# A windowed-attention and gated-MLP kernel on one core: where the Wo products stand, which steps carry the norms, and how the first loads are cut

## The chip, the cores and the metric

The kernel runs on one core of one Trainium2 chip. The metric is the device time of one execution in microseconds (us). Besides that time, one execution was recorded by the hardware profiler; its records are called the profile or the trace here.

## The reference

```
x  = A_x                                     # [2048, 512], bf16
xn = (x - mean(x)) / sqrt(var(x) + 1e-5)     # over the last axis
# A: causal attention with a window of 256 keys, 32 heads of 16
q, k, v = split(xn @ wqkv)                   # wqkv [512, 1536]
p  = softmax(q k^T / 4, masked where not 0 <= i - j < 256)
a  = (p v) @ wo                              # wo [512, 512]
# B: a gated product without a nonlinearity
b  = ((xn @ w_gate) * (xn @ w_up)) @ w_down  # F = 1792
out = x + a + b                              # [2048, 512]
```

B_x is not used.

## The kernel before, in words

The 2048 rows are cut into four chunks of 512, T = 0 to 3, and a chunk into four blocks of 128 rows, b = 0 to 3. All weights and x stay in SBUF. For a chunk the kernel makes the norm of its blocks, transposes them (`xnT`), projects V, K and Q (`vp`, `qkp`), makes gate and up products for 14 groups of 128 hidden columns (`gp`, `up`, and their product `hT`), the scores and exponentials of the attention, and the products of the weights with V (`acc`). The last two products add into one PSUM tile per block: `psd` takes 14 matmuls of `down` (L375: hT with Wd) and then four of `wo` (L381: OT with Wo, one for each group c of eight heads). `store` (L399) adds x on VectorE (DVE) and issues the copy to HBM.

The order is written out by the program itself. There are 76 score steps: 16 for chunk 0 and 20 for each later one, four or five steps for each pair (T, c). A step is `scores` (matmuls into the one S tile, L258; an exponential on ScalarE (ACT), L265; triangular masks on GpSimd (POOL), L137), then, where a pair (T, c) ended two steps earlier, `values` (the acc matmuls, L313, and two DVE transposes, L319) and `divide` (DVE: reciprocal, product L331, and the transpose L333 that writes `OT`), then `fill`, then `mask_diag` (DVE, L286).

`fill` takes the next items of a list, `fillers()`, as long as a budget lasts. The budget rises by 14.24 units with each step; a unit is about one matmul of 512 columns, scores cost 1.85 units, values 5.5. An item of the list may carry `after`: it may not be taken before that pair has been divided in an earlier step, and then the list stops:

```
cost, f, before, after = work[n]
if after is not None and after > valued:
    break
```

In chunk T the list holds, for b = 0 to 3, the `down` items of block b of chunk T-1 (seven items of two matmuls), `wo` with c = 0, 1, `wo` with c = 2, 3, and the store; then the gate and up items of chunk T and the projections of chunk T+1. Between the blocks stand the norm items of chunk T+1, at cost 0: `norm_stats` (DVE, L148, L149), `norm_scale` (POOL: `ve` L157, `rs` L159), `norm_apply` (DVE, L167), `norm_transpose` (a DMA transpose on the SP queue, L179). Chunk 1's norms stand between the gate and up items of chunk 0. PSUM has four banks for everything but the scores (tag M), among them `psd`, `acc`, `gp`, `up`, `vp`, `qkp`. A tile of that tag gets the bank that was freed first.

The start (`setup`, `first_chunk`): SP issues the loads of x block 0, block 1, blocks 2 and 3 together, then Wqkv in three parts of 512 columns (V, K, Q), then the other weights. TensorE (PE) multiplies an identity 42 times (`wps`, L89) while it has no data. DVE takes, in this order, the statistics of blocks 0 and 1, and then for each b the apply of block b and the statistics of block b + 2. POOL makes ve and rs. PE takes the transposes of block 0 (`xTp`, L183), and then for each b the transposes of block b + 1 and the V projection of block b. ACT copies each transposed block to `xnT` (L184) and each V block out of PSUM (L201).

Of the kernel before, what the change touches and what calls it, by code (L numbers as in the profile page):

```python
# [10 lines left out]
ACT = mybir.ActivationFunctionType  # L11
ALU = mybir.AluOpType
# [13 lines left out]
class Kernel:  # L26
# [26 lines left out]
    def setup(self):  # L53
        nc, const, NT, NF = self.nc, self.const, self.NT, self.NF
        self.x = const.tile([128, NT, 512], BF16, name="x")
        self.Wqkv = const.tile([128, 4, 1536], BF16, name="Wqkv")
        self.Wo = const.tile([128, 4, 512], BF16, name="Wo")
        self.Wg = const.tile([128, 4, self.F], BF16, name="Wg")
        self.Wu = const.tile([128, 4, self.F], BF16, name="Wu")
        self.Wd = const.tile([128, NF, 512], BF16, name="Wd")  # L60
        xv = self.x_d.rearrange("(t p) d -> p t d", p=128)
        wq = self.w_d["qkv"].rearrange("(k p) n -> p k n", p=128)
        wg = self.w_d["g"].rearrange("(k p) n -> p k n", p=128)
        wu = self.w_d["u"].rearrange("(k p) n -> p k n", p=128)
        for lo, hi in ((0, 1), (1, 2), (2, 4)):
            nc.sync.dma_start(out=self.x[:, lo:hi, :], in_=xv[:, lo:hi, :])
        for lo in (1024, 512, 0):
            nc.sync.dma_start(out=self.Wqkv[:, :, lo:lo + 512], in_=wq[:, :, lo:lo + 512])
        h = self.F // 2
        for lo in (0, h):  # L70
            nc.sync.dma_start(out=self.Wg[:, :, lo:lo + h], in_=wg[:, :, lo:lo + h])
            nc.sync.dma_start(out=self.Wu[:, :, lo:lo + h], in_=wu[:, :, lo:lo + h])
            if lo == 0:
                nc.sync.dma_start(out=self.x[:, 4:8, :], in_=xv[:, 4:8, :])
        nc.sync.dma_start(out=self.Wd[:], in_=self.w_d["d"].rearrange("(f p) n -> p f n", p=128))
        nc.sync.dma_start(out=self.Wo[:], in_=self.w_d["o"].rearrange("(c p) n -> p c n", p=128))
        nc.sync.dma_start(out=self.x[:, 8:NT, :], in_=xv[:, 8:NT, :])

        warm = const.tile([128, 1], F32, name="warm")
        nc.vector.memset(warm[:], 0.0)  # L80
        nc.scalar.activation(out=warm[:], in_=warm[:], func=ACT.Exp)
        ident = const.tile([128, 128], BF16, name="ident")
        nc.gpsimd.memset(ident[:], 0.0)
        nc.gpsimd.affine_select(out=ident[:], in_=ident[:], compare_op=ALU.not_equal, fill=1.0,
                                base=0, pattern=[[-1, 128]], channel_multiplier=1)
        self.ident = ident
        wps = self.ps_m.tile([128, 128], F32, tag="M", name="wps")
        for _ in range(42):
            nc.tensor.matmul(wps[:], lhsT=ident[:], rhs=ident[:], start=True, stop=True)  # L89
        pi = const.tile([128, 1], I32, name="pi")  # L90
        nc.gpsimd.iota(pi[:], pattern=[[0, 1]], base=0, channel_multiplier=1)
        podd = const.tile([128, 1], I32, name="podd")
        nc.vector.tensor_scalar(out=podd[:], in0=pi[:], scalar1=4, scalar2=1,
                                op0=ALU.arith_shift_right, op1=ALU.bitwise_and)
        self.odd = const.tile([128, 1], F32, name="odd")
        nc.vector.tensor_copy(out=self.odd[:], in_=podd[:])
        self.mhalf = const.tile([128, 4], F32, name="mhalf")
        nc.gpsimd.memset(self.mhalf[:], -0.5)
        self.diag = const.tile([128, 64], BF16, name="diag")
        self.far = const.tile([128, 64], BF16, name="far")  # L100
        nc.gpsimd.memset(self.diag[:], BIG)
        nc.gpsimd.memset(self.far[:], BIG)
        for half in (slice(0, 64), slice(64, 128)):
            self.triangle(self.diag[half], True)
            self.triangle(self.far[half], False)
        self.xnT, self.Q, self.hT, self.O, self.OT = {}, {}, {}, {}, {}
        self.K, self.Ko, self.V, self.VS = {}, {}, {}, {}
        self.strips, self.at = {}, {}
# [43 lines left out]
    def norm_scale(self, t, n=4):  # L152

        nc = self.nc
        mv = self.stats[t][0]
        ve = self.small.tile([128, n], F32, tag="ve", name="ve")
        nc.gpsimd.tensor_scalar(out=ve[:], in0=mv[:, :, 1], scalar1=1e-5, scalar2=None, op0=ALU.add)  # L157
        rs = self.small.tile([128, n], F32, tag="rs", name="rs")
        nc.gpsimd.tensor_tensor(out=rs[:], in0=ve[:], in1=self.mhalf[:, 0:n], op=ALU.pow)  # L159
        for u in range(t, t + n):  # L160
            self.stats[u][2] = rs
# [9 lines left out]
    def norm_transpose(self, t, by_dma):  # L171

        nc = self.nc
        xn = self.xns.pop(t)
        T, b = divmod(t, 4)
        if b == 0:
            self.xnT[T] = self.chunk2.tile([128, 4, 4, 128], BF16, tag="xnT", name=f"xnT{T}")
        if by_dma:
            nc.sync.dma_start_transpose(out=self.xnT[T][:, b, :, :], in_=xn[:])  # L179
            return  # L180
        ps = self.ps_m.tile([128, 4, 128], BF16, tag="M", name="xTp")
        for k in range(4):
            nc.tensor.transpose(ps[:, k, :], xn[:, 128 * k:128 * k + 128], self.ident[:])  # L183
        nc.scalar.activation(out=self.xnT[T][:, b, :, :], in_=ps[:], func=ACT.Copy)  # L184

    def bank(self, ks, name):

# [37 lines left out]
    def first_chunk(self):  # L225

        self.new_chunk(0)
        for b in range(2):
            self.norm_stats(b, 1)
            self.norm_scale(b, 1)  # L230
        for b in range(4):
            self.norm_apply(b)
            if b < 2:
                self.norm_stats(b + 2, 1)
                self.norm_scale(b + 2, 1)
        self.norm_transpose(0, False)
        for b in range(4):
            if b < 3:
                self.norm_transpose(b + 1, False)
            self.proj_v(b)  # L240
        self.proj_qk(0, 0, 1)
        self.proj_qk(0, 0, 0, on_act=True)
        self.swap_halves(0, self.nc.scalar)
        self.proj_qk(0, 1, 1)
# [158 lines left out]
    def fillers(self):  # L403


        out = []
# [30 lines left out]
        def norms(T, at, step):  # L437

            t, out = 4 * T, {}
            for b in range(4):  # L440
                for k, f in enumerate((lambda b=b: self.norm_stats(t + b, 1),
                                       lambda b=b: self.norm_scale(t + b, 1),
                                       lambda b=b: self.norm_apply(t + b),
                                       lambda b=b: self.norm_transpose(t + b, True))):
                    out.setdefault(at + step * b + (0, 0, 1, 1)[k], []).append((0, f))
            return out

        def down(T, b):
            for lo in range(0, NF, 2):
                add(2, lambda lo=lo: self.down(T, b, lo, lo + 2))  # L450

        def wo(T, b, cs):
# [3 lines left out]
        for c in range(2, 4):  # L456
            qk(0, c, self.first[0, c])
        for T in range(NCH):
            todo = {}
            if T:  # L460
                todo = norms(T + 1, 0, 1) if T + 1 < NCH else {}
                for b in range(4):
                    for g in todo.get(b, ()):
                        add(*g)
                    down(T - 1, b)
                    wo(T - 1, b, (0, 1))
                    wo(T - 1, b, (2, 3))
                    add(0, lambda T=T, b=b: self.store(T - 1, b))
            for g in todo.get(4, ()):
                add(*g)  # L470
            gu(T, norms(1, 1, 3) if T == 0 else {})
            if T + 1 < NCH:
                project(T + 1)
# [9 lines left out]
    def run(self):  # L483
# [12 lines left out]
                    steps.append((T, c, pieces))  # L496
        due = {g: key for key, g in self.last.items()}
        SCORES, VALUES = 1.85, 5.5
        work = self.fillers()
        total = sum(w[0] for w in work) - RESERVE + SCORES * len(steps) + VALUES * (len(due) - 1)  # L500
        spent, n, scored = 0, 0, 0
# [29 lines left out]
        for g, s in enumerate(steps):  # L531
            fill(-1, g)
            valued = ready
            self.scores(*s)
            scored = spent
            spent += SCORES
            upto = total * (g + 1) / len(steps)
            if values(g - LAG):
                fill(min(spent + 4, upto), g)
                divide(g - LAG)  # L540
            if g < len(steps) - 1:
                fill(upto, g)
                self.mask_diag(*s)
# [57 lines left out]
```

The softmax here doesn't subtract the row's maximum and nothing guards it: scores larger than these inputs give would overflow.

## Time and profile before

| what | value |
|---|---|
| median of 3 runs | 273.40 us (273.21 to 273.44) |
| the profiled execution's own time | 273.34 us |
| its span, first to last instruction | 271.6 us |
| PE busy | 261.7 us, 96% of the span |
| DVE, ACT, POOL busy | 182.3, 170.6, 113.4 us |
| granted TensorE clock, mean | 1.000 |

The span leaves out what lies before the first and after the last instruction: 273.34 - 271.6 = 1.74 us. Times in the trace are counted from the start of the span. Matmuls overlap: one of 512 columns is recorded with about 380 ns, while the next starts 215 ns after it (four vp matmuls are recorded with 1.02 us together). So the ends of PE work are modelled, and an idle time after a matmul is recorded somewhat shorter than the time that was lost.

### The profile page before, as it was taken

Reading aid. Unit: us, or ns where it says so; the run is one execution under the profiler, and the core shown is the slowest. Engines: PE = TensorE matmul, PEld = TensorE weight load, DVE = VectorE, ACT = ScalarE, POOL = GpSimd, SP = SyncE. Lnnn points to the kernel's source line nnn. Section 1 sums busy time; section 2 is a strip of 40 time slices with the busy share of each in tenths; the row PEclk is TensorE's granted clock in tenths of the full one; section 3 lists DMA queues with packets and bytes.
Section 4 is the critical chain, followed back from the end, with each engine's and each line's share of the span. In section 5 each row is a group of like instructions: output and inputs, shape, how many; then the busy total and the mean of one; then the engine's idle time right before and its main releaser. Section 6 shows DMA issues by size and latency. Waiting matters only on the chain.

```text
span 271.6 us, 8888 instructions
## 1 busy us (share of the span) xinstructions
PE 261.7 (96%) x3886; PEld 120.2 (44%) x3886; DVE 182.3 (67%) x351; ACT 170.6 (63%) x131; POOL 113.4 (42%) x282
## 2 busy tenths in 40 slices
PE   7999999999799999999989999999999999999993
PEld 6444444444344444444434444444444444444452
DVE  5377998876845959676665868857662675969160
ACT  3666757686456676769655676768765666675400
POOL 6123333434545443345545543545443354443400
PEclk9999999999999999999999999999999999999999
DMA  6999911110021100001012110000200000000001
GB/s 197 365 350 344 243 21 22 23 46 0 28 55 41 39 2 4 2 2 43 5 39 72 31 22 2 0 4 2 46 9 32 24 21 2 2 0 6 0 24 57
DMA packets 19351, 15.12 MB, mean 56 GB/s; under 512 B 7152, under 2 KB 19312, under 8 KB 19312
## 3 DMA queue, kind: packets, MB, share of 16 engines
q1 hardware_dynamic: 18480, 14.06, 17.9%
q8 instruction: 30, 0.49, 0.8%
q10 hardware_dynamic: 832, 0.49, 0.6%
q14 instruction: 9, 0.07, 0.1%
HBM read 9.70 MB, written 2.10 MB: 43 GB/s over the span
## 4 chain that ended last, share of the span: by engine, by line
PE 86%; DVE 9%; DMA 2%; ACT 1%; SPq 0%; issue 0%; POOL 0%; DVEq 0%; POOLq 0%
PE gp L342 17%; PE up L356 17%; PE psd L375 16%; PE qkp L209 10%; PE S L258 9%; PE acc L313 6%; PE psd L381 4%; PE vp L197 4%; DVE at L319 2%; DMA Wqkv<-in_A_wqkv_dram 2%; DVE hT L360 1%; DVE OT L333 1%; DVE on L331 1%; PE L L375 1%; DVE gsb L350 1%; ACT P L265 1%
## 5 line engine op out<-in xcount | busy, mean ns | idle before, releaser
L265 ACT ACTIVATE P<-S 128x2048 bf16<-128x2048 f32 x76 | 141.0, 1855 | 60.6 <-PE S L258 56.9
L137 POOL TENSOR_SCALAR_AFFINE_SELECT P<-P 64x256 bf16<-64x256 bf16 x224 | 96.8, 432 | 127.8 <-ACT P L265 117.2
L342 PE MATMUL gp<-xnT,Wg 128*128 128x512 bf16 x224 | 60.0, 380 | 0.1
L356 PE MATMUL up<-xnT,Wu 128*128 128x512 bf16 x224 | 59.6, 380 | 0.0
L375 PE MATMUL psd<-Wd,hT 128*128 128x512 bf16 (+1 forms) x210 | 50.3, 373 | 0.0
L360 DVE TENSOR_TENSOR hT<-up,gsb 128x512 bf16<-128x512 f32 x56 | 38.4, 686 | 16.3 <-PE up L356 14.4
L286 DVE TENSOR_TENSOR P<-P,diag 128x512 bf16<-128x512 bf16 (+1 forms) x76 | 30.6, 404 | 11.1 <-ACT P L265 11.1
L375 PEld LDWEIGHTS <-hT 128*128 128x128 bf16 x238 | 22.0, 98 | 24.4 <-issue 2.8
L319 DVE STREAM_TRANSPOSE at<-acc 128x512 f32<-128x512 f32 x30 | 19.7, 695 | 19.3 <-PE acc L313 19.3
L258 PE MATMUL S<-Q,K 16*64 16x320 bf16 (+2 forms) x720 | 31.1, 260 | 0.6 <-ACT P L265 0.5
L356 PEld LDWEIGHTS <-Wu 128*128 128x128 bf16 x224 | 20.4, 98 | 25.3 <-issue 2.5
L342 PEld LDWEIGHTS <-Wg 128*128 128x128 bf16 x224 | 20.3, 98 | 25.5 <-issue 2.7
L258 PE MATMUL S<-Q,Ko 32*64 32x320 bf16 (+1 forms) x720 | 31.1, 260 | 0.0
L209 PE MATMUL qkp<-xnT,Wqkv 128*128 128x512 bf16 x128 | 30.0, 380 | 0.0
L258 PEld LDWEIGHTS <-K 16*64 16x64 bf16 x720 | 12.3, 103 | 32.7 <-issue 32.7
L350 DVE CAST gsb<-gp 128x512 bf16<-128x512 f32 x36 | 24.5, 682 | 2.4 <-PE gp L342 1.0
L348 ACT ACTIVATE gsb<-gp 128x512 bf16<-128x512 f32 x20 | 11.9, 597 | 12.2 <-PE gp L342 11.5
L313 PE MATMUL acc<-P,VS 64*32 64x320 bf16 (+4 forms) x672 | 18.9, 254 | 0.0
L381 PE MATMUL psd<-Wo,OT 128*128 128x512 bf16 (+1 forms) x60 | 16.4, 374 | 2.5 <-DVE OT L333 2.5
L313 PE MATMUL acc<-P,V 64*32 64x320 bf16 (+4 forms) x672 | 18.4, 254 | 0.5 <-DVE hT L360 0.5
L209 PEld LDWEIGHTS <-Wqkv 128*128 128x128 bf16 x128 | 11.7, 98 | 14.5 <-issue 1.4
L399 DVE TENSOR_TENSOR y<-psd,x 128x512 bf16<-128x512 f32 x13 | 8.9, 688 | 13.3 <-PE psd L381 13.1
(54 smaller groups left out, 201.4 us busy)
## 6 DMA issues: line engine op xcount, KB each, us to landing
Wg<-in_B_w_gate_dram SPq DMA_DIRECT2D x2, 896.0 KB, 11.5
Wu<-in_B_w_up_dram SPq DMA_DIRECT2D x2, 896.0 KB, 12.8
Wd<-in_B_w_down_dram SPq DMA_DIRECT2D x1, 1792.0 KB, 17.6
out_dram<-y SPq DMA_DIRECT2D x14, 128.0 KB, 1.7
Wqkv<-in_A_wqkv_dram SPq DMA_DIRECT2D x3, 512.0 KB, 6.4
x<-in_A_x_dram SPq DMA_DIRECT2D x1, 1024.0 KB, 10.3
VS<-V SPq DMA_DIRECT2D x6, 144.0 KB, 2.6
x<-in_A_x_dram SPq DMA_DIRECT2D x1, 512.0 KB, 11.2
```

The lines of the kernel that those rows point to most:

```text
L137: nc.gpsimd.affine_select(out=v, in_=v, pattern=pattern + [[1 if diag else -1, 64]], compare_op=ALU.is_ge if diag else ALU.is_gt, fill=0.0 ...
L209: nc.tensor.matmul(ps[:], lhsT=self.Wqkv[:, k, lo:lo + 128], rhs=self.xnT[T][:, :, k, :], start=(k == 0), stop=(k == 3))
L258: nc.tensor.matmul(S[64 * par:64 * par + 64, e, col:col + n], lhsT=(self.Ko if par else self.K)[U][rows, c, keys], rhs=self.Q[T][rows, c, ...
L265: nc.scalar.activation(out=P[:, :, 0:col], in_=S[:, :, 0:col], func=ACT.Exp, scale=0.25)
L286: self.nc.vector.tensor_tensor(out=v, in0=v, op=ALU.min, in1=self.diag.unsqueeze(1).unsqueeze(1).to_broadcast([128, 4, n, 64]))
L313: nc.tensor.matmul(accs[par][32 * e:32 * e + 32, q:q + n], lhsT=v, rhs=P[rows, e, col:col + n], start=(i == 0), stop=(i == len(todo) - 1), ...
L342: nc.tensor.matmul(ps[:], lhsT=self.Wg[:, k, 128 * f:128 * f + 128], rhs=self.xnT[T][:, :, k, :], start=(k == 0), stop=(k == 3))
L350: nc.vector.tensor_copy(out=self.gsb[:], in_=ps[:])
L356: nc.tensor.matmul(ps[:], lhsT=self.Wu[:, k, 128 * f:128 * f + 128], rhs=self.xnT[T][:, :, k, :], start=(k == 0), stop=(k == 3))
L360: nc.vector.tensor_tensor(out=self.hT[T][:, f, :], in0=ps[:], in1=self.gsb[:], op=ALU.mult)
L375: nc.tensor.matmul(ps, lhsT=self.hT[T][:, f, 128 * b:128 * b + 128], rhs=self.Wd[:, f, c0:c1], start=(f == 0), stop=False)
L381: self.nc.tensor.matmul(ps, lhsT=self.OT[T][:, c, 128 * b:128 * b + 128], rhs=self.Wo[:, c, c0:c1], start=False, stop=(c == 3))
```

## The change

It has five parts.

1. In the list, six of the seven `down` items of block b + 1 now stand ahead of `wo` c = 2, 3 and the store of block b; the seventh and `wo` c = 0, 1 of block b + 1 follow behind the store. Two psd tiles are open at a time.
2. The norms of chunks 2 and 3 leave the list. They are tied to the score steps 0, 2, 3, 4 and 5 of chunk T (`beside`), issued after that step's values and divide and ahead of its fill and its mask_diag.
3. The loads at the start: x in four blocks of 128 rows; the V part of Wqkv in two halves (the 128-row groups k = 0, 1 and k = 2, 3), between x blocks 1 and 2 and between x blocks 2 and 3. K and Q follow as before.
4. 38 warm-up matmuls in place of 42.
5. For block 0 alone, `ve` on DVE in place of POOL; for the first block of a chunk that is transposed on PE (block 0 of chunk 0), the copy to xnT in two halves.

```diff
-        for lo, hi in ((0, 1), (1, 2), (2, 4)):
-            nc.sync.dma_start(out=self.x[:, lo:hi, :], in_=xv[:, lo:hi, :])
-        for lo in (1024, 512, 0):
+        for b in range(4):
+            nc.sync.dma_start(out=self.x[:, b:b + 1, :], in_=xv[:, b:b + 1, :])
+            if b in (1, 2):
+                ks = slice(2 * b - 2, 2 * b)
+                nc.sync.dma_start(out=self.Wqkv[:, ks, 1024:1536], in_=wq[:, ks, 1024:1536])
+        for lo in (512, 0):
             nc.sync.dma_start(out=self.Wqkv[:, :, lo:lo + 512], in_=wq[:, :, lo:lo + 512])
...
-        for _ in range(42):
+        for _ in range(38):
             nc.tensor.matmul(wps[:], lhsT=ident[:], rhs=ident[:], start=True, stop=True)
...
-        nc.gpsimd.tensor_scalar(out=ve[:], in0=mv[:, :, 1], scalar1=1e-5, scalar2=None, op0=ALU.add)
+        (nc.gpsimd if t else nc.vector).tensor_scalar(out=ve[:], in0=mv[:, :, 1], scalar1=1e-5, scalar2=None,
+                                                      op0=ALU.add)
...
-        nc.scalar.activation(out=self.xnT[T][:, b, :, :], in_=ps[:], func=ACT.Copy)
+        for ks in (slice(0, 2), slice(2, 4)) if b == 0 else (slice(0, 4),):
+            nc.scalar.activation(out=self.xnT[T][:, b, ks, :], in_=ps[:, ks, :], func=ACT.Copy)
...
-        def down(T, b):
-            for lo in range(0, NF, 2):
+        def down(T, b, part=range(0, NF, 2)):
+            for lo in part:
                 add(2, lambda lo=lo: self.down(T, b, lo, lo + 2))
...
-            todo = {}
             if T:
-                todo = norms(T + 1, 0, 1) if T + 1 < NCH else {}
+                if T + 1 < NCH:
+                    for i, fs in norms(T + 1, 0, 1).items():
+                        self.beside[self.first[T, 0] + (0, 2, 3, 4, 5)[i]] = fs
+                down(T - 1, 0)
+                wo(T - 1, 0, (0, 1))
                 for b in range(4):
-                    for g in todo.get(b, ()):
-                        add(*g)
-                    down(T - 1, b)
-                    wo(T - 1, b, (0, 1))
+                    if b < 3:
+                        down(T - 1, b + 1, range(0, NF - 2, 2))
                     wo(T - 1, b, (2, 3))
                     add(0, lambda T=T, b=b: self.store(T - 1, b))
-            for g in todo.get(4, ()):
-                add(*g)
+                    if b < 3:
+                        down(T - 1, b + 1, range(NF - 2, NF, 2))
+                        wo(T - 1, b + 1, (0, 1))
...
+            for _, f in self.beside.get(g, ()):
+                f()
             if g < len(steps) - 1:
                 fill(upto, g)
                 self.mask_diag(*s)
```

## The prediction

> **What bounds the kernel now.** I read the page first (busy shares and the chain of waits), then the list of waits of TensorE alone, then the timeline around each wait in it, and the start last.
>
> ```profile
> PE 261.7 (96%) x3886; PEld 120.2 (44%) x3886; DVE 182.3 (67%) x351; ACT 170.6 (63%) x131; POOL 113.4 (42%) x282
> ...
> PE 86%; DVE 9%; DMA 2%; ACT 1%; SPq 0%; issue 0%; POOL 0%; DVEq 0%; POOLq 0%
> ```
>
> PE is the bound: busy for 96% of the span and 86% of the chain. The change removes four warm-up matmuls and no other PE work, so it can only win idle time of PE. The waits of PE say how much there is.
>
> ```profile
> PE psd L381 <- DVE OT L333: 2.5, 3, 1.5
> PE wps L89 <- POOL ident L84: 1.4, 1, 1.4
> PE S L258 <- ACT P L265: 0.5, 1, 0.5
> PE acc L313 <- DVE hT L360: 0.5, 1, 0.5
> PE xTp L183 <- DVE xn L167: 0.4, 1, 0.4
> ```
>
> The first row is what the reordering aims at: a Wo product that waits for OT. Two of its three places lie in the middle:
>
> ```profile
> 68.31 0.60 PE L381 MATMUL psd<-Wo,OT 128*128 128x512 bf16 x2
> 69.42 0.25 PE L258 MATMUL S<-Q,K 16*64 16x128 bf16 x4 [0.51 <-ACT P L265]
> ...
> 69.78 0.39 PE L381 MATMUL psd<-Wo,OT 128*128 128x512 bf16 x1
> 71.66 0.39 PE L381 MATMUL psd<-Wo,OT 128*128 128x512 bf16 x1 [1.49 <-DVE OT L333]
> 71.89 1.46 PE L375 MATMUL psd<-Wd,hT 128*128 128x512 bf16 x6
> ```
>
> Here the list has stopped (`after`): step 17 gives PE only two Wo products behind its acc, so step 18's scores come early and wait for the exponential of step 17, then Wo c = 3 waits for the OT that DVE is still making.
>
> ```profile
> 135.58 0.82 PE L381 MATMUL psd<-Wo,OT 128*128 128x512 bf16 x3
> 137.12 0.39 PE L381 MATMUL psd<-Wo,OT 128*128 128x512 bf16 x1 [0.72 <-DVE OT L333]
> ```
>
> The same at step 38. In chunk 3 the down products begin a step later and nothing waits. The third place, at 262.4 us, is the end, which the change leaves alone.
>
> The start:
>
> ```profile
> 4.77 0.41 DVE L167 TENSOR_SCALAR xn<-x,mv,rs 128x512 bf16<-128x512 bf16 x1 [0.20 <-POOL rs L159]
> 5.54 0.27 PEld L183 LDWEIGHTS <-xn 128*128 128x128 bf16 x4
> 6.21 0.69 DVE L148 BATCH_NORM_STATS2 st<-x 128x6 f32<-128x512 bf16 x1
> 6.35 0.40 PE L183 MATMUL xTp<-ident,xn 128*128 128x128 bf16 x4 [0.37 <-DVE xn L167]
> 6.85 1.02 PE L197 MATMUL vp<-Wqkv,xnT 128*128 128x512 bf16 x4
> ```
>
> The first projection starts at 6.85; the V weights landed at 2.19 + 4.62 = 6.81 (the chain's DMA piece), while the transposes before it could have let it go at 6.35 + 4 x 0.055 = 6.57. From 6.85 on PE is full.
>
> **Part 1, Wo behind down.** The lost time is counted from starts, since ends are modelled. Chunk 1: two Wo from 68.31, 0.215 each, then scores about 0.1 later (as at 66.68, 66.99), so 68.84; they came at 69.42: 0.58 lost. The Wo at 69.78 frees PE at 70.00; the next started at 71.66: 1.66 lost. Chunk 2: three Wo from 135.58 end at 136.22; the next came at 137.12: 0.90 lost. Sum 3.14 us (2.72 as recorded idle).
>
> With the change, the planner's budget (14.24 a step, less 1.85 and, in a values step, 5.5) puts this at steps 17 and 18: acc, Wo c = 0, 1, four down products of block 1; scores; eight more down products; then Wo c = 2, 3. From 68.31: 6 x 0.215 gives 69.60; the exponential of step 17 is over at 67.49 + 1.88 = 69.37, so scores no longer wait; they take 0.36 + 0.1, so 70.06; eight products, 71.79. OT was usable at 71.66. It fits by 0.13 us: if DVE is later, that lateness is lost one for one. In chunk 2 Wo c = 2, 3 falls into step 39, 12 products and a score step later: no wait. No PE instruction is added. Gain 3.14.
>
> What pays: two psd tiles are open instead of one, of four banks. Banks go to the next tile in the order in which they were freed; while psd 0 and 1 are open, the two acc banks, freed at step 17 (37), serve psd 2 and 3. The banks of psd 0 and 1 are first wanted by the acc of step 22 (42), two steps after their stores. Cover: that distance. If it went, each store that PE must await costs its 0.69 us and more (rival C).
>
> **Part 2, norms on steps.** The same DVE and POOL instructions and DMA transposes, moved by less than two steps. xnT of the next chunk is read only by its projections, over 40 us later, so their lateness is hidden, as is that of the transposes and y copies in SP's queue (1.2 and 0.4 us each). The cost is queueing. On POOL, ve and rs (0.22 + 0.57) follow the step's triangles, which wait for its exponential; four of them take 1.99. So rs comes up to 1.99 + 0.9 = 2.9 us after the exponential. The apply stands one step later at the head of DVE, with its wait; mask_diag of the step before is done some 0.6 us after the exponential. So DVE can stand idle for 1.3 to 2.3 us in steps 19, 20, 21 and 39, 40, 41, where before it had the y store to do first and met no such wait. Behind it stand stats (0.69 + 0.18), the y store, and mask_diag. Who waits for those: mask_diag is read by values two or more steps later, the store's bank see above. DVE has room: 2.1 of 4 us busy in 72 to 76. Cost on the path: 0, bounds 0 and 1.5 us; nearest row: no PE wait on y in the before.
>
> **Parts 3 to 5, the start.** Warm-up: 42 weight loads in 4.16 us are 0.099 each, so four fewer free PE 0.40 earlier, at 5.18 instead of 5.58. ve on DVE: 0.15 (a 128x1 DVE operation at 1.50) in place of POOL's 0.22 with hand-over: xn of block 0 comes at about 5.1 instead of 5.18, but stats of block 1 move back by 0.15. Two half copies cost ACT about 0.2 more, beside the next transposes: nothing waits for it. So block 0 is transposed at 5.2, block 1 at about 6.4 (before 6.35: DVE's order is unchanged), and the first projection can go at 6.63 instead of 6.85, if V is there.
>
> V now lands in two halves: blocks 2 and 3, second in line with the same bytes, landed at 1.72 + 2.9 = 4.6; V, 512 KB behind them, at 6.81. In the new order the same megabyte ends with x block 3. Spread over 4.6 to 6.81, the first V half lands at 4.6, x block 2 at 5.15, the second V half at 6.2, x block 3 at 6.8; at the 369 GB/s of 4.6 to 5.6 it would be 6.1. Statistics of block 3 started at 6.21 from data that had landed at 4.6; now they are the last to land, and the apply of block 2 is behind them on DVE: 0.87 + 0.4 us later, then the transpose of block 2, which PE takes ahead of its V product. At 6.1 the start gains 0.3 us; at 6.8 PE waits 0.5 for block 2 and about 0.3 is lost by the fourth V product (before at 10.13), through rs (0.57), apply and the copies. I take 0, the middle.
>
> Two rules weigh on this. Row: x blocks of 128 KB landed in 2.0 to 2.3 us. The Trainium skill (DMA: Bandwidth & Descriptors, Anatomy of one DMA) gives 2 us fixed plus bytes at 436 GB/s, for its other DMA path: 2.3 us. By it alone x block 3, sixth on SP at 0.80 + 5 x 0.465 = 3.1, would land at 5.4, and the sum would be 0.3 us better. The trace's V row (4.6 us from issue, 3.2 by the rule) shows that queued bytes decide; I follow it. K and Q are issued two SP slots (0.9 us) later with the same bytes ahead; K landed near 9.1 and is used at 11.0.
>
> Row: the granted clock reads 1.00 throughout, yet warm-up matmuls step at 0.099 us and transposes of the same width at about 0.055. The skill (TensorE: Matmul & The Clock Gate, Part 1) says that PE runs at half clock until some 3.4 us of activity in a window that runs free. Against this change: 38 matmuls are 3.8 us, and a window that straddles the idle spots at 6 us could keep the half clock to about 8.2. That would cost about half of 5.2 to 8.2 less idle time, 1.2 us. The trace had reached full pace by the last warm-ups, before 5.6, so I take 0 and keep 1.2.
>
> **The sum.** 273.34 (profiled execution) - 3.14 + 0 + 0 = 270.2; the median of the runs is 0.06 above that execution, so 270.3.
>
> **Rivals.**
> A, as above: 270.3; own range 269.4 to 271.0 (recorded idle alone, -2.72; start -0.5 to +0.3).
> B, x block 3 lands later than V did, or the half clock stays: start +0.7 to +1.2, 271.0 to 271.5. For: it is last in line, and DVE and PE both take it in order. Against: the bytes are the same.
> D, the Wo wait stays in chunk 1, since OT is late by a microsecond or more behind DVE's work: 271.3 to 272.6. For: the slack is 0.13 us. Against: the norms come behind the divide.
> C, slower: apply waits at the head of DVE for rs, and PE for the store behind it. At six steps, 1.3 us each reach PE if a psd bank must be reused in the next step: 7.8 - 3.1 = +4.7, so 278. It decides from 0.5 us per step on. Against: the banks' order.
>
> **How the numbers follow.** A 0.69, B 0.14, D 0.09, C 0.08. About 0.2% (0.55 us) is what a measurement of this kernel can tell from no change. A, B and nearly all of D are faster: 0.89; the end of D and a mild C are the same: 0.05; C slower: 0.06. The range 269.4 to 271.9 holds A, B and half of D.
>
> **What would show it.** No PE wait on OT near 70 and 137; scores at 69.6 without a wait for P; PE busy unchanged but for 0.4 us. DVE waits of xn on rs longer than the 1.0 us of before, and no PE wait on y. First vp near 6.6; the wait of st on x of block 3, and xTp of blocks 2 and 3 behind it. PE waits on DVE y or psd in 72 to 84 would make me wrong to the slow side.

## The result, and the profile after

| what | before | after |
|---|---|---|
| median, measured on one chip, 4 runs each | 273.42 us | 270.26 us (270.07 to 270.94) |
| ratio after / before, 95% interval | | 0.9887 [0.9866, 0.9908] |
| profiled execution, own time | 273.34 us | 270.28 us |
| its span | 271.6 us | 268.6 us |

The forecast was 270.3 us. The total agrees; the terms below it do not all agree, and that is what the experiments are about. In some kernels of this case, before among them, a part of the executions took about 2 us more than the rest; medians, ranges and ratios include them (only the ratio of e2 leaves out its two slowest), so that the ratios of the experiments can lie 0.002 below those of the medians.

The page of after, first its busy row and the shares of its chain of waits, then the whole list of waits of TensorE (columns: who waits for whom, us in total, times, longest):

```profile
PE 261.5 (97%) x3882; PEld 120.0 (45%) x3882; DVE 181.6 (68%) x352; ACT 170.8 (64%) x132; POOL 113.8 (42%) x281
...
PE 87%; DVE 7%; DMA 2%; ACT 1%; SPq 1%; issue 1%; POOL 0%; DVEq 0%; POOLq 0%
```

```profile
PE wps L92 <- POOL ident L87: 1.4, 1, 1.4
PE xTp L187 <- DVE xn L171: 1.3, 2, 1.1
PE psd L386 <- DVE OT L338: 0.3, 1, 0.3
```

PE is busy for nearly as long as before and the span is shorter: idle time was won, not work. Of the three waits on OT only the one at the end is left, S no longer waits for P, and, not foreseen, the wait of acc on hT is gone too. The wait of xTp on xn has grown from 0.4 to 1.3 us.

Chunk 1, in the timeline (start, duration, engine, line, operation):

```profile
68.92 0.60 PE L386 MATMUL psd<-Wo,OT 128*128 128x512 bf16 x2
...
69.36 1.03 PE L380 MATMUL psd<-Wd,hT 128*128 128x512 bf16 x4
...
70.32 0.25 PE L263 MATMUL S<-Q,K 16*64 16x128 bf16 x4
...
70.68 1.90 PE L380 MATMUL psd<-Wd,hT 128*128 128x512 bf16 x8
...
71.51 0.71 DVE L338 STREAM_TRANSPOSE OT<-on 128x512 bf16<-128x512 bf16 x1
...
72.42 0.59 PE L386 MATMUL psd<-Wo,OT 128*128 128x512 bf16 x2
```

This is the predicted order: two Wo, four down, scores, eight down, two Wo. OT was usable at about 72.28 (as before, 0.06 us after its record ends), and the Wo product came at 72.42: the slack is 0.14 us, the forecast said 0.13. Chunk 2 runs as worked out, too: two Wo, twelve down, a score step, two Wo. OT was done there at about 135.5, some 2 us before it was wanted:

```profile
133.96 0.61 PE L386 MATMUL psd<-Wo,OT 128*128 128x512 bf16 x2
134.40 2.75 PE L380 MATMUL psd<-Wd,hT 128*128 128x512 bf16 x12
...
137.45 0.60 PE L386 MATMUL psd<-Wo,OT 128*128 128x512 bf16 x2
```

The start of after:

```profile
5.45 0.63 PE L187 MATMUL xTp<-ident,xn 128*128 128x128 bf16 x4
...
6.56 1.04 PE L202 MATMUL vp<-Wqkv,xnT 128*128 128x512 bf16 x4
...
7.45 0.69 DVE L151 BATCH_NORM_STATS2 st<-x 128x6 f32<-128x512 bf16 x1 [1.20 <-DMA x<-in_A_x_dram]
...
8.27 0.38 DVE L171 TENSOR_SCALAR xn<-x,mv,rs 128x512 bf16<-128x512 bf16 x1
...
8.71 0.40 PE L187 MATMUL xTp<-ident,xn 128*128 128x128 bf16 x4 [1.12 <-DVE xn L171]
8.95 1.03 PE L202 MATMUL vp<-Wqkv,xnT 128*128 128x512 bf16 x4
...
10.12 2.06 PE L202 MATMUL vp<-Wqkv,xnT 128*128 128x512 bf16 x8
...
12.02 1.67 PE L214 MATMUL qkp<-xnT,Wqkv 128*128 128x512 bf16 x7
```

The first V product starts earlier than before (6.56 against 6.85), as forecast at 6.6. But DVE stands for 1.20 us before the statistics of block 3, the apply of block 2 (8.27) stands behind them, PE waits 1.12 for it, and the first K product comes at 12.02, where in before it came at 11.01:

```profile
11.01 1.67 PE L209 MATMUL qkp<-xnT,Wqkv 128*128 128x512 bf16 x7
```

Where the time went is read best from one event that both kernels have at every score step: the start of the step's exponential on ACT. After less before, in the two profiled executions:

| score steps | after - before, us | change in this stretch |
|---|---|---|
| 1 to 9 | +1.01 | +1.01, the start |
| 10 to 17 | +0.61 | -0.40, the wait of acc on hT |
| 19 | -1.62 | -2.24, Wo in chunk 1 |
| 39 to the end of PE | -2.52 | -0.89, Wo in chunk 2 |
| end of the span | -3.07 | -0.55, between the end of PE's work and the end of the span |

### The profile page after: what moved, and what is told of

Read it like the earlier page. It is cut to its first block, busy times and chain, and to the rows that moved or that the text cites. A ratio compares the mean times of both kernels' runs of the same rounds, so it can differ in the third digit from the quotient of the medians.

```text
span 268.6 us, 8884 instructions
## 1 busy us (share of the span) xinstructions
PE 261.5 (97%) x3882; PEld 120.0 (45%) x3882; DVE 181.6 (68%) x352; ACT 170.8 (64%) x132; POOL 113.8 (42%) x281
## 4 chain that ended last, share of the span: by engine, by line
PE 87%; DVE 7%; DMA 2%; ACT 1%; SPq 1%; issue 1%; POOL 0%; DVEq 0%; POOLq 0%
PE up L361 17%; PE psd L380 17%; PE gp L347 17%; PE qkp L214 11%; PE S L263 9%; PE acc L318 6%; PE psd L386 5%; PE vp L202 4%; DMA x<-in_A_x_dram 2%; DVE at L324 1%; DVE hT L365 1%; PE L L380 1%; DVE gsb L355 1%; DVE st L151 1%; ACT P L270 1%
## 5 line engine op out<-in xcount | busy, mean ns | idle before, releaser
L380 PE MATMUL psd<-Wd,hT 128*128 128x512 bf16 (+1 forms) x210 | 51.1, 373 | 0.0
L263 PE MATMUL S<-Q,K 16*64 16x320 bf16 (+1 forms) x720 | 31.1, 260 | 0.1
L318 PEld LDWEIGHTS <-V 64*32 64x32 bf16 x720 | 14.5, 90 | 2.8 <-issue 2.4
```

Of the source, the lines that this page charges most:

```text
L263: nc.tensor.matmul(S[64 * par:64 * par + 64, e, col:col + n], lhsT=(self.Ko if par else self.K)[U][rows, c, keys], rhs=self.Q[T][rows, c, ...
L318: nc.tensor.matmul(accs[par][32 * e:32 * e + 32, q:q + n], lhsT=v, rhs=P[rows, e, col:col + n], start=(i == 0), stop=(i == len(todo) - 1), ...
L380: nc.tensor.matmul(ps, lhsT=self.hT[T][:, f, 128 * b:128 * b + 128], rhs=self.Wd[:, f, c0:c1], start=(f == 0), stop=False)
```

## The experiments

Eleven runs were made, in three groups; each group has runs of before on its own chip beside it (medians 273.49, 273.71 and 273.46). "Shift" is the table's measure: step for step against before, in profiled executions.

**e1, Wo behind down alone.** The norms stay in the list, between the blocks.

```diff
...
+                for g in todo.get(0, ()):
+                    add(*g)
+                down(T - 1, 0)
+                wo(T - 1, 0, (0, 1))
                 for b in range(4):
-                    for g in todo.get(b, ()):
-                        add(*g)
-                    down(T - 1, b)
-                    wo(T - 1, b, (0, 1))
+                    if b < 3:
+                        down(T - 1, b + 1, range(0, NF - 2, 2))
                     wo(T - 1, b, (2, 3))
                     add(0, lambda T=T, b=b: self.store(T - 1, b))
+                    if b < 3:
+                        for g in todo.get(b + 1, ()):
+                            add(*g)
+                        down(T - 1, b + 1, range(NF - 2, NF, 2))
+                        wo(T - 1, b + 1, (0, 1))
```

> Part 1 alone on the kernel before; the norms stay in the list, between the blocks; the start is the old one. My theory: the whole gain is the Wo wait, lost time 2.24 us at steps 17 to 18 and 0.90 at step 38; so 273.4 - 3.1 = 270.3, perhaps 269.9 if DVE does not hold back an instruction at 36.5 us as it did in the execution before (0.4 us). Rival (both order changes are needed, since norms in the list hold the stores or Wo back): less than 2.5 us gained, and a PE wait on OT or y left near 70 or 137.

Measured: 270.60 us (270.57 to 270.96), ratio 0.9876 [0.9844, 0.9907], span 268.8. The shift is +0.03 at the start, -2.21 at step 19 and -3.10 at step 40: the gain of part 1, by itself. Then 0.52 is given back between steps 44 and 45. The list of PE's waits of this kernel names it, and the timeline shows the place:

```profile
PE up L356 <- DVE y L399: 0.5, 1, 0.5
PE acc L313 <- DVE hT L360: 0.5, 1, 0.5
```

```profile
149.17 0.40 DVE L167 TENSOR_SCALAR xn<-x,mv,rs 128x512 bf16<-128x512 bf16 x1
...
149.48 0.69 DVE L148 BATCH_NORM_STATS2 st<-x 128x6 f32<-128x512 bf16 x1
...
150.65 0.69 DVE L331 TENSOR_TENSOR on<-at,rz 128x512 bf16<-128x512 f32 x1
...
151.38 0.71 DVE L333 STREAM_TRANSPOSE OT<-on 128x512 bf16<-128x512 bf16 x1
...
152.02 0.40 DVE L286 TENSOR_TENSOR P<-P,diag 128x512 bf16<-128x512 bf16 x1
...
152.34 0.68 DVE L399 TENSOR_TENSOR y<-psd,x 128x512 bf16<-128x512 f32 x1
...
153.07 1.02 PE L356 MATMUL up<-xnT,Wu 128*128 128x512 bf16 x4 [0.47 <-DVE y L399]
```

The last store of the chunk stands on DVE behind the divide and the mask, and ahead of the divide stand an apply and the statistics of a norm (about 1.1 us of DVE). The bank that the store frees is the one that `up` wants. This is a late store that holds PE, as in rival C, once and for 0.5 us, but in a kernel without part 2. In after no norm stands at that place: the store runs from 151.80 to 152.48, before `up` is due at 153.12, and PE has no such wait.

**e5, norms tied to steps alone.**

```diff
-                todo = norms(T + 1, 0, 1) if T + 1 < NCH else {}
+                if T + 1 < NCH:
+                    for i, fs in norms(T + 1, 0, 1).items():
+                        self.beside[self.first[T, 0] + (0, 2, 3, 4, 5)[i]] = fs
...
+            for _, f in self.beside.get(g, ()):
+                f()
```

> Part 2 alone on the kernel before: the norms of chunks 2 and 3 tied to score steps, the list's order and the start unchanged. My prediction: DVE stands waiting for rs in steps 19 to 21 and 39 to 41 (some 7 us in all instead of 1.0), and none of it reaches PE: 273.4 as before, between 273.2 and 273.8, with the Wo waits of 2.5 us still there. The slower rival: stores and masks behind the waiting apply hold PE: a PE wait on y, psd or mask, and 274 or more.

Measured: 273.67 us (273.15 to 275.38), ratio 0.9995 [0.9968, 1.0022]. DVE's wait for rs in before and in e5, then PE's waits in e5:

```profile
DVE xn L167 <- POOL rs L159: 1.0, 2, 0.8
```

```profile
DVE xn L167 <- POOL rs L159: 9.1, 8, 2.7
```

```profile
PE psd L381 <- DVE OT L333: 2.5, 3, 1.5
...
PE S L258 <- ACT P L265: 0.5, 1, 0.5
PE acc L313 <- DVE hT L360: 0.5, 1, 0.5
```

DVE waits 9.1 us in total at the applies, where before it waited 1.0, and PE's waits in the middle are those of before to the tenth. The shift is +0.35 at step 1 and +0.37 at the end, so all but 0.02 of it lies ahead of the norms of chunks 2 and 3. Here long waits on an engine that has room cost nothing.

**e2, the start alone (parts 3 to 5).** The edit is the first four pieces of the diff shown with the change.

> Parts 3 to 5 alone on the kernel before (loads in four x blocks and V halves, 38 warm-ups, ve on DVE, halved first copy). My theory: x block 3 lands last, near 7 us, so the transpose of block 2 comes late and everything from the first K product on moves back by 0.7 to 1.0 us: 274.1 to 274.4. Rival (the start is neutral, as predicted, and the late landing in the profile was one execution's chance): 273.2 to 273.6, with x block 3 landing before 6.6.

Measured: 273.92 us (273.08 to 277.71), ratio 1.0016 [0.9993, 1.004]. x block 3 is used at 7.66 and the first K product starts at 12.24; the shift is +1.23, then +0.79 from step 10 on. Block 3 is as late as expected, but the median is below the expected 274.1. By itself the new start gains nothing: in the profile the work of PE ends 0.8 us later than in before, the span only 0.2 us later.

**e3, after with the loads of before.** Parts 1, 2, 4 and 5 stay.

```diff
-        for b in range(4):
-            nc.sync.dma_start(out=self.x[:, b:b + 1, :], in_=xv[:, b:b + 1, :])
-            if b in (1, 2):
-                ks = slice(2 * b - 2, 2 * b)
-                nc.sync.dma_start(out=self.Wqkv[:, ks, 1024:1536], in_=wq[:, ks, 1024:1536])
-        for lo in (512, 0):
+        for lo, hi in ((0, 1), (1, 2), (2, 4)):
+            nc.sync.dma_start(out=self.x[:, lo:hi, :], in_=xv[:, lo:hi, :])
+        for lo in (1024, 512, 0):
```

> The changed kernel with the loads of before (x in 1, 1, 2 blocks, then V whole); warm-up, ve and the halved copy stay changed. If the loads cost the start its 1.0 us: first V product again near 6.85 with the landing of V, first K product near 11.0, and 270.3 - 1.0 = 269.2. If the shorter warm-up (a later clock) costs it: no better than 270.0.

Measured: 269.65 us (269.48 to 269.88), ratio 0.9837 [0.9803, 0.9871]. First V product at 6.87, first K product at 11.20. The shift is +0.19, then -0.40 at step 10, and -3.35 at the end, which is 0.19 - 0.40 - 2.24 - 0.89 to within 0.01. So part 3 is what costs time in after: without it the kernel is 0.6 us below after's median, where 1.0 was expected, and the two ranges do not touch.

**e4 and e11, the V halves behind all of x.** The same kernel, run in two groups: after, with x in 1, 1 and 2 blocks and then V in its two halves. Of the edit, the lines that come in:

```diff
+        for lo, hi in ((0, 1), (1, 2), (2, 4)):
+            nc.sync.dma_start(out=self.x[:, lo:hi, :], in_=xv[:, lo:hi, :])
+        for ks in (slice(0, 2), slice(2, 4)):
+            nc.sync.dma_start(out=self.Wqkv[:, ks, 1024:1536], in_=wq[:, ks, 1024:1536])
         for lo in (512, 0):
```

> The changed kernel with x in 1, 1, 2 blocks and then V in its two halves. The first half lands with 768 KB before 6.2, so the first V product starts near 6.6 and nothing of x is late: 269.0, 0.2 below the run with V whole. If the order of the transposes and not the landing of V bounds the start: the same as with V whole, 269.2.

> The kernel with V in halves behind x once more, as the version to keep, beside the others of this set. 269.5 (269.1 to 270.0), some 0.8 below the changed kernel; first K product near 11.1.

Measured: e4 269.53 us (269.11 to 270.34), ratio 0.9836 [0.9804, 0.9869]; e11 269.04 us (268.85 to 269.79), ratio 0.9826 [0.9783, 0.9868]. The start of e11:

```profile
6.62 0.59 PE L201 MATMUL vp<-Wqkv,xnT 128*128 128x512 bf16 x2
...
7.70 0.59 PE L201 MATMUL vp<-Wqkv,xnT 128*128 128x512 bf16 x2 [0.48 <-DMA Wqkv<-in_A_wqkv_dram]
...
11.43 2.32 PE L213 MATMUL qkp<-xnT,Wqkv 128*128 128x512 bf16 x10
```

The second V half landed at 7.65 here and at 7.37 in e4, about as late as x block 3 in after (7.42). But what is late is now used by PE at once: from that landing to the first K product it is 3.77 us in e4 and 3.78 in e11, against 12.02 - 7.42 = 4.60 in after. So the work behind the last load counts, and not only when it lands. These are the fastest kernels of the case. Against e3, with the V weights in one piece, the halves show no clear gain: e4 and e3 ran on one chip and their ranges overlap.

**e6, after once more**, unchanged, on the chip of e7, e8 and e9.

> The changed kernel once more, for a second profile and beside the others of this set. 270.3 (270.0 to 270.9). x block 3 lands last again: if near 7.4, first K product near 12.0; if it lands by 6.6, that product comes before 11.3 and the run is near 269.6, and the late landing was chance.

Measured: 270.43 us (270.09 to 271.0), ratio 0.9864 [0.9829, 0.9899]. In its profiled execution (271.0) x block 3 landed at 8.30 and the first K product came at 12.90. So the landing itself moves by about 0.9 us between executions, and DVE and PE follow it: from the landing to the first K product it is 4.60 us in after, e2, e6 and e8 alike.

**e9, the apply of block 2 ahead of the statistics of block 3.** The prediction's path for the loss was that order on DVE.

```diff
+            if b == 3:
+                self.norm_stats(3, 1)
+                self.norm_scale(3, 1)
...
-            if b < 2:
-                self.norm_stats(b + 2, 1)
-                self.norm_scale(b + 2, 1)
+            if b == 0:
+                self.norm_stats(2, 1)
+                self.norm_scale(2, 1)
```

> The changed kernel with the apply of block 2 ahead of the statistics of block 3 on DVE. My prediction's account of the start: x block 3's lateness reaches PE through the apply of block 2, which stands behind its statistics; then the V product of block 1 comes near 7.8 instead of 8.95, and the start wins back 0.5 or more: 269.8. Rival: block 3's own chain (statistics, ve, rs, apply, transpose, copy, V product) from its landing sets the first K product; then the V products of blocks 1 and 2 come earlier and the first K product stays near 12.0: 270.3.

Measured: 269.78 us (269.38 to 270.07), ratio 0.9838 [0.9803, 0.9872]. The second V product comes at 8.28 instead of 8.95, but the first K product at 12.30, with block 3 landed at 7.94. From landing to K it is 4.36 us against 4.60 in after and e6: the order is worth 0.24 us at the first K product. The rest is block 3's own chain, as the rival had it:

```profile
7.96 0.69 DVE L151 BATCH_NORM_STATS2 st<-x 128x6 f32<-128x512 bf16 x1 [0.39 <-DMA x<-in_A_x_dram]
...
9.87 0.41 DVE L171 TENSOR_SCALAR xn<-x,mv,rs 128x512 bf16<-128x512 bf16 x1 [1.00 <-POOL rs L163]
10.34 0.40 PE L187 MATMUL xTp<-ident,xn 128*128 128x128 bf16 x4 [1.03 <-DVE xn L171]
```

Statistics, ve and rs on POOL, apply, transpose, copy, V product: all of that lies behind the last load. The median is 0.65 below e6's on the same chip, more than 0.24; the landing varies by as much, so the surplus is not assigned.

**e7 and e8, one DVE instruction more or less.** In after, e2, e3 and e4 the wait of acc on hT had gone; in before, e1 and e5 it stood. The four have `ve` of block 0 on DVE in common, one instruction more in DVE's program, 30 us earlier. e7 is before with one idle DVE instruction in the setup; e8 is after with that `ve` back on POOL.

```diff
+        spare = const.tile([128, 1], F32, name="spare")
+        nc.vector.memset(spare[:], 0.0)
```

```diff
-        (nc.gpsimd if t else nc.vector).tensor_scalar(out=ve[:], in0=mv[:, :, 1], scalar1=1e-5, scalar2=None,
+        nc.gpsimd.tensor_scalar(out=ve[:], in0=mv[:, :, 1], scalar1=1e-5, scalar2=None,
```

> The kernel before with one more instruction on DVE in the setup (a memset of a column that nothing reads). In the profiles so far the hT product of chunk 0 near 36.5 us started 0.46 us after its last semaphore in the two kernels whose ve is on POOL alone, and at once in the four whose DVE program has one instruction more. Theory: it is the place of that instruction in DVE's program; then the hold is gone, and 273.4 - 0.4 = 273.0. Rival: it is the timing of the start; then the hold stays, and 273.4.

> The changed kernel with ve of block 0 back on POOL (DVE's program one instruction shorter, all else as changed). If the hold on DVE goes with the number of its instructions: it is back, 270.3 + 0.4 = 270.7. If ve on DVE was worth its hand-over alone: the first V product 0.1 later, the end unmoved because x block 3 sets it, 270.3.

Measured: e7 273.09 us (272.68 to 274.99), ratio 0.9988 [0.9966, 1.0011]; e8 270.73 us (270.4 to 271.62), ratio 0.988 [0.9841, 0.9919]. The times are too close to tell 0.4 us, the timelines are not. The gp product on PE and the hT product on DVE follow the same last up product. In before, then after, then e7, then e8:

```profile
36.50 1.02 PE L342 MATMUL gp<-xnT,Wg 128*128 128x512 bf16 x4
36.96 0.69 DVE L360 TENSOR_TENSOR hT<-up,gsb 128x512 bf16<-128x512 f32 x1 [0.51 <-DVE gsb L350]
```

```profile
37.52 1.02 PE L347 MATMUL gp<-xnT,Wg 128*128 128x512 bf16 x4
37.57 0.69 DVE L365 TENSOR_TENSOR hT<-up,gsb 128x512 bf16<-128x512 f32 x1
```

```profile
36.87 1.02 PE L344 MATMUL gp<-xnT,Wg 128*128 128x512 bf16 x4
36.92 0.69 DVE L362 TENSOR_TENSOR hT<-up,gsb 128x512 bf16<-128x512 f32 x1
```

```profile
37.83 1.02 PE L347 MATMUL gp<-xnT,Wg 128*128 128x512 bf16 x4
38.29 0.69 DVE L365 TENSOR_TENSOR hT<-up,gsb 128x512 bf16<-128x512 f32 x1 [0.52 <-DVE gsb L355]
```

hT starts 0.46 us behind gp in before and in e8, and 0.05 behind it in after and e7. The profile names DVE's own gsb as what it waited for, which was long done. One DVE instruction more takes the hold away and one less brings it back; e7's shift drops by 0.40 from step 9 to 10, and e8 has again `acc` waiting 0.5 for hT. The rival, the timing of the start, is out: ahead of that place e5 and e7 are shifted alike, by +0.36 and +0.37, and only e5 has the hold.

**e10, e4 with 12 warm-up matmuls.**

```diff
-        for _ in range(38):
+        for _ in range(12):
```

> The kernel with V in halves behind x (269.5), with 12 warm-up matmuls in place of 38. PE then has nothing to do between 2.7 and 5.3 us. If the clock opens by a window of some 3.4 us that has to be busy: it opens at 8.5 to 12 us, the transposes and the first V and K products run at half pace, and 270.5 to 271.5. If the clock opens at a fixed time: no change, 269.5.

Measured: 270.87 us (270.36 to 271.69), ratio 0.989 [0.9854, 0.9925], 1.8 us above e11 on the same chip and 1.3 above e4 on another. Its first V products:

```profile
6.82 2.05 PE L201 MATMUL vp<-Wqkv,xnT 128*128 128x512 bf16 x4
...
12.44 1.24 PE L213 MATMUL qkp<-xnT,Wqkv 128*128 128x512 bf16 x5
```

The first two V products start 0.42 us apart (6.82, 7.24), in e11 0.22; of the 2.05 us of the four, a part is the wait for the second half of V, which landed at 7.81. K starts a microsecond later than in e11. In the trace's clock records full pace begins at 9.64 here; in the kernels with 38 or 42 warm-ups it began between 4.83 and 7.20. So it does not begin at a fixed time, and the expectation with a window is met.

## Why the prediction was right, and where it was not

**Wo behind down: right in mechanism, place and size.** Forecast 2.24 in chunk 1 and 0.90 in chunk 2; measured 2.24 and 0.89 both in after and in e1, which has part 1 alone. It came from counting lost time from the starts of matmuls, which gave 3.14, where recorded idle time gave 2.72. The order at steps 17 and 18 and the slack of 0.13 us came out as worked from the planner's budget. Rival D is out.

**Norms on steps: cost 0 on the path, shown by e5.** DVE's waits for rs were forecast at 1.3 to 2.3 us in three steps of two chunks; in after they measured 1.27, 1.74 and 0.27 in chunk 1 and 1.74, 1.27 and 0.27 in chunk 2, so the third was mis-sized; in e5 they reach from 0.27 to 2.70. What the prediction did not see is that part 1 needs company: with the norm items where e1 put them, a store came late once and cost 0.52. Part 1 and part 2 together give 3.13, part 1 alone about 2.6. Other places for the norms in the list were not tried.

**The start: the term that failed.** The prediction took 0, "the middle" between a gain of 0.3 and a loss of 0.3; the profiles show +1.01 in after, +1.23 in e2, +1.90 in e6. The path that it named, the apply of block 2 behind the statistics of block 3 and the transpose behind that, is the one that PE waits on in after; but e9 shows that this order is worth only 0.24 us at K, and that block 3's own chain up to its V product, which the prediction named last, sets the rest. The number that was wrong is the landing of x block 3: taken at 6.1 to 6.8, with the argument that the same megabyte ends when it ended before. It landed at 7.42, 7.64, 8.30, 7.74 and 7.94 in after, e2, e6, e8 and e9. So the end of the last V bytes before, 6.81, is not the end of the last bytes when they are cut into more pieces: in e4, e10 and e11, too, the megabyte ended at 7.37 to 7.81, while with the loads of before it ended at 6.39 to 6.83 in five traces. Why is open: each further load also takes about 0.5 us to issue, so the last piece is issued at about 2.2 in before, 2.7 in e4 and 3.2 in after, and no run parts this from the cutting. With the true landing the prediction's own sum gives 0.3 + (7.42 - 6.8) = 0.9, near the measured 1.01. Rival B named this case, at +0.7 to +1.2 and with a chance of 0.14.

The figure of the Trainium skill (DMA: Bandwidth & Descriptors, Anatomy of one DMA) that was set aside gave, as an estimate, 5.4 for block 3. Setting it aside was right, and the correction too small: in the five traces the block took 4.23 to 5.13 us from its issue at about 3.2.

**The clock: taken at 0, right on the path.** Full pace began at 6.00 in after, behind the transposes of block 0 (0.63 us for four, 0.39 in before), but before the V products. In e3 it began at 7.20 and the first four V products took 1.20 us in place of 1.02. But four warm-ups fewer are not shown to be the reason: with 42, it began at 5.26 in before, and at 6.35 and 7.09 in e5 and e7, whose starts are 0.36 us later than that of before, though e5 changes nothing of the start and e7 only adds an idle DVE instruction. So a shift of a few tenths at the start can be one execution's. The kept risk of 1.2 us was real in kind, and e10 shows its size when the warm-up is cut much further: 1.0 us between the profiled executions (270.56 and 269.56), 1.3 to 1.8 us between medians.

**Why the total still came out: luck.** -3.14 + 1.01 is -2.13, or 271.2. Two things not in the sum made it 270.28: -0.40 by the hold on hT, which e7 and e8 tie to the number of DVE instructions, an accident of part 5; and -0.55 between the end of PE's work and the end of the span. Without them it would have been rival B's 271.2, still inside the range that the prediction gave. The last stores were issued at 267.72 in before and 265.21 in after, and the spans end 3.9 and 3.4 us later; in e6, which is after again, it was 3.2, in e1 3.7. No part of the change touches the instructions of this last stretch. Yet in the thirteen traces it is 3.7 to 3.9 us in the five kernels with the loads of before (before, e1, e3, e5, e7) and 2.6 to 3.5 in the eight with other loads, on each of the three chips of the experiments. So it seems to go with part 3, which would give back at the end a part of what it costs at the start; why is open, and each run has one trace only.

## What to carry to other kernels

When loads are reordered at a start, count what must still be done behind the load that lands last: 128 KB of x behind V carried a chain of 4.6 us to the next projection, half of V behind x carried 3.8. A fill order is better planned by the starts of work on the bound engine than by its recorded idle time, and an engine with room could wait here for microseconds at no cost, as long as nothing that the bound engine wants stands behind it. A right total is no proof of its terms: shifts step by step between two traces show each term for itself.

## What the runs showed of the hardware that was not expected

A DVE instruction can be held by 0.46 us with everything that it waits for done, and whether it is depends on how many instructions the engine's program has before it: one more on DVE took 0.40 us off the path of before (e7), one less put it back (e8). In the traces a load of the instruction queue falls at 37.7 to 39.1 us in the four kernels with the hold and at 31.3 to 32.4 us in the nine without. That the load has to do with the hold is not shown.

The half clock came back in one profiled execution, that of e7 (274.81 us). A table of stretches of e7, then the same of before (us, then busy time of PE, PEld, DVE, ACT, POOL, then the granted clock, the DMA share and GB/s):

```profile
68.00:72.00 4.00, 1.78 (x60) 0.88 (x45) 3.39 (x6) 3.21 (x2) 1.31 (x4) 0.99 0.02 6
72.00:76.00 4.00, 4.00 (x13) 1.49 (x11) 2.11 (x5) 0.00 (x0) 2.42 (x6) 0.58 0.24 66
```

```profile
68.00:72.00 4.00, 2.00 (x69) 0.92 (x45) 3.39 (x6) 3.24 (x2) 1.30 (x4) 1.00 0.02 6
72.00:76.00 4.00, 4.00 (x42) 1.67 (x40) 2.11 (x5) 0.02 (x1) 2.44 (x6) 1.00 0.27 66
```

In both, PE was idle for about half of the 4 us around the Wo wait of chunk 1, in no single recorded wait of more than 1.5 us. In e7 the clock then fell to half from 71.94 to 75.35, and the shift against before grew by 1.69 us from step 18 to 19; in before it stayed. What differs is where the wait lies between the times at which the clock can change. In all thirteen traces a stretch between two changes of the clock lasts a whole multiple of 3.413 us (one for the fall in e7, 19 and 58 on its two sides, 76 to 78 in the other traces). On this grid the 3.41 us right ahead of the fall, 68.52 to 71.94, have PE busy for 1.20 us, or 35%. In before, e5 and e2 the same wait lies across two such windows, each busy for 55% or more. The rule of the Trainium skill (TensorE: Matmul & The Clock Gate, Part 1) asks for an idle window of about 3.4 us; this one was busy for a third of its length.

The mean clock of the other executions fits. One window at half clock lowers the mean to 0.994, and the executions near 275 us of before (23 of 73), e5 (4 of 14), e7 (10 of 22) and e2 (4 of 22) read 0.993 or 0.994. Four of e2, near 277 us, read 0.987 or 0.988, as two such windows would; where the second lies is on no trace. The kernels without the Wo wait show no reading under 0.997 in 51 executions. No kernel was run to try this, so the share of a window below which the clock falls stays open.
